# Cosine by the half angle, a shorter float64 conversion, and no whole tiles on GpSimd, in a fused attention and MoE kernel

## The chip, the core and the metric

The kernel runs on one core of a Trainium2 chip. Five engines with queues of their own are used: TensorE (PE for products, PEld for loading their stationary operand), VectorE (DVE), ScalarE (ACT), GpSimd (POOL) and SyncE (SP, which issues all transfers here). Each works through its instructions in the order in which they were issued, and they wait for each other at semaphores. The metric is the time of one execution on the device in microseconds.

## The reference

```python
def _attn_ref(q, k, v, g_norm):                       # float32, batch 8, 8 heads, 576 rows, 64 wide
    kv = np.einsum('bhsd,bhse->bhde', k, v)
    out = np.einsum('bhsd,bhde->bhse', q, kv)
    rms = np.sqrt(np.mean(out * out, axis=-1, keepdims=True) + 1e-06)
    return (out / rms * g_norm).astype(np.float32)

def _moe_ref(x, w_in, w_out):                         # x: 4608 x 512 (the heads side by side)
    h = x @ w_in                                      # w_in: 512 x 2048, float64
    g = h * np.cos(h)
    return (g @ w_out).astype(np.float32)             # w_out: 2048 x 512, float64
```

The weights reach the kernel as float64, the rest as float32.

## The kernel before

The 4608 tokens are cut into 12 chunks of 384, the 2048 hidden columns into 16 tiles of 128. A *step* is one such tile for one chunk: 192 steps. A step multiplies w_in's tile with the chunk's x (stage 1, into a PSUM bank `ps_h`), computes g = h cos(h) from it (`act_part`), and multiplies g with w_out's tile (stage 2, into three PSUM banks `acc`). Every float32 operand of the large products is split into a high part in float32r and a low part (the remainder), and three products are summed: so a step has 12 products of 384 columns into `ps_h` and 9 of 512 columns into `acc`. The names tell the parts: `xhi`/`xlo`, `ghi`/`glo`, and for a weight tile `wi` or `wo` its two halves `w[:, 0]` and `w[:, 1]`.

Four places matter here.

*Weights* (`w_part`, 32 tiles of 128x512). A tile lands as 64-bit words. DVE scales and clamps the low word (`m`), joins it by a shift and an or with the high word, and fixes sign and exponent bits. ACT makes the sign of the value from the high word in two operations (`sg`). The product of the two is the float32 value; ACT casts it to the high half, and the remainder is subtracted. Product and subtraction go to DVE or to POOL.

*Cosine* (`act_part`, per step). ACT makes `ki`, h over 2 pi plus a quarter, rounded to an integer by the int32 output. DVE subtracts ki times 2 pi in two parts (`r`), and clamps r. ACT takes the sine of r plus pi/2, DVE multiplies with h, ACT casts to `ghi`, and DVE or POOL subtracts to `glo`.

*x* (`x_part`, `kv_part`). For each chunk and pair of heads q is multiplied with k-transposed-v (`kv`) and normalised; the reciprocal root is a power on POOL (`rinv`) in a tile of 128x6 or 128x12. The remainders `qlo`, `xlo` and, for the early kv, `kv_lo` go to DVE or POOL. The first two chunks take a path with fewer transfers.

*Output* (`out_part`). ACT copies `acc` to SBUF and it is stored. The first two chunks use the first 8 tiles of the hidden columns, both of them, before the other 8, so their partial sums go out and come back, and DVE adds them.

The order of all instructions is made by a planner (`Order`) when the program is built: each part says which engine it needs next and for how long, the planner simulates the engines and issues an instruction when its simulated engine takes it; the lowest priority number goes first. Where a part names two engines, the one that would be done first is taken. `either(f, bias)` is such a choice between DVE and POOL:

```python
    def either(f, bias=0.0):
        return [("DVE", 0.067 + f / 960, bias), ("POOL", 0.15 + f / 480, 0.0)]
```

On the chip the order is fixed, the times are what they are. Every instruction is recorded by one helper, so the profile has line 190 for nearly all of them, and rows are told apart by their tiles.

Of the kernel before, what the change touches and what calls it, by code (L numbers as in the profile page):

```python
# [19 lines left out]
P = 128  # L20
# [29 lines left out]
class Order:  # L50
    """Puts the program's parts in an order by a simulation of the engines.

    A part of the program is a generator. It yields what it needs next: ("run", [(engine, us), ...], prio)
    for the use of one of these engines, ("wait", events) or ("take", tokens). After a "run" it issues its
    instructions, in the order in which the simulated engines start them; the lowest prio goes first.
    """
# [7 lines left out]

    def spawn(self, gen, t=0.0):
        self.advance(Proc(gen, t), None)

# [72 lines left out]
def tile_kernel(  # L140
# [271 lines left out]
    def kv_split_part(b, p, prio):  # L412
        """The parts of an early kv, for a chunk that isn't."""
# [3 lines left out]
        e, end = yield "run", either(P), prio  # L417
        by_name[e].tensor_tensor(
# [19 lines left out]
    def x_part(c, p, prio):  # L438
# [24 lines left out]
        else:  # L463
# [4 lines left out]
            e, end = yield "run", either(CH), prio  # L468
            by_name[e].tensor_tensor(out=qlo, in0=qT, in1=qhi.bitcast(F32), op=ALU.subtract)
# [85 lines left out]
        e, end = yield "run", either(CH), prio  # L555
        by_name[e].tensor_tensor(out=xlo[:, p, :], in0=x, in1=xhi[:, p, :].bitcast(F32), op=ALU.subtract)
# [4 lines left out]
    def w_part(key, prio):  # L561
        yield "wait", [w_in[key]]
        yield "take", t_wst
        sign_done = Event()
# [34 lines left out]
        e, end = yield "run", either(DM, 1.5), prio  # L599
        by_name[e].tensor_tensor(out=w[:, 1, :], in0=sg, in1=w[:, 0, :].bitcast(F32), op=ALU.subtract)  # L600
# [39 lines left out]
    def act_part(i, h):  # L640
        prio = due(i + 2) - 4.0
        yield "take", t_ki
        yield "run", [("ACT", 0.37)], prio
# [3 lines left out]
        yield "run", [("DVE", 0.47)], prio  # L647
        r = ew.tile([P, CH], F32, name="r")
        dve.scalar_tensor_tensor(out=r, in0=ki, scalar=-C1, in1=h, op0=ALU.mult, op1=ALU.add)
        _, end = yield "run", [("DVE", 0.47)], prio  # L650
        dve.scalar_tensor_tensor(out=r, in0=ki, scalar=-C2, in1=r, op0=ALU.mult, op1=ALU.add)
        sched.give(t_ki, end)
        yield "run", [("DVE", 0.27)], prio
        dve.tensor_scalar(
            out=r, in0=r, scalar1=-R_MAX - PI / 2, scalar2=R_MAX - PI / 2, op0=ALU.max, op1=ALU.min)
        yield "run", [("ACT", 0.51)], prio
        act.activation(out=r, in_=r, func=AF.Sin, bias=half_pi)
        _, end = yield "run", [("DVE", 0.47)], prio
# [3 lines left out]
        yield "run", [("ACT", 0.41)], prio  # L662
# [153 lines left out]
```

## Time and profile before

| what | value |
|---|---|
| times of three runs | 936.47, 937.34, 938.5 us (median 937.34) |
| profiled execution | span 933.4 us, first to last instruction; its own time is shown as this span alone |
| PE busy | 898.7 us (96%) |
| DVE busy | 722.4 us (77%) |
| ACT busy | 487.0 us (52%) |
| POOL busy | 221.2 us (24%), 105.4 of them powers |
| granted TensorE clock | 0.985 in the mean |

A row of a group reads: line, engine, operation, output and inputs by name, shape and type, count, then busy us and mean ns of one, then the idle time before them and what ended it. A row of the timeline reads: start in us, duration in us, engine, line, operation, names, shapes, count. A row of the waits reads: the engine and the tile that waited, for whom, us in total, times, longest.

### The profile page before, as it was taken

The page shows a single profiled execution, that of the slowest core. Times are in us where ns is not written, and L with a number is a line of the kernel's source. Part 1 is how long each engine was busy: PE and PEld are TensorE (multiplying, and loading weights), DVE is VectorE, ACT ScalarE, POOL GpSimd, SP SyncE. Part 2 cuts the span into 40 slices and gives each one's busy share as a digit, 9 for nine tenths or more (in the row PEclk, how much of TensorE's full clock was granted, in tenths as well). Part 3 has the DMA queues.
Part 4 walks back from the last instruction along what each step waited for, and adds up shares of the span by engine and source line. Part 5 has one row for each costly group of instructions (what it writes and reads, how often), then busy time and mean ns, then how long its engine had stood idle before and what let it go on. Part 6 is the DMA issues. An engine that isn't in the chain of part 4 may idle for free.

```text
span 933.4 us, 14111 instructions
## 1 busy us (share of the span) xinstructions
PE 898.7 (96%) x5008; PEld 798.7 (86%) x5008; DVE 722.4 (77%) x1442; ACT 487.0 (52%) x1094; POOL 221.2 (24%) x148
## 2 busy tenths in 40 slices
PE   8797878999999999999999999999999999999998
PEld 6685666889889998888889999889889999999997
DVE  3999999799777777777776876786886886886664
ACT  5876666455445445455445545454553653653443
POOL 3676655122120220121120220210210220220000
PEclk7899999999999999999999999999999999999999
DMA  9997001153211102121220111220310110100000
GB/s 253 261 314 233 35 0 57 18 161 99 68 42 43 18 9 69 43 60 47 58 67 25 27 18 30 72 69 9 94 18 1 51 18 1 52 1 1 35 1 34
DMA packets 112246, 58.59 MB, mean 63 GB/s; under 512 B 80432, under 2 KB 103984, under 8 KB 112176
## 3 DMA queue, kind: packets, MB, share of 16 engines
q1 hardware_dynamic: 112176, 57.70, 22.9%
q8 instruction: 39, 0.64, 0.3%
q14 instruction: 31, 0.25, 0.1%
HBM read 46.66 MB, written 11.01 MB: 62 GB/s over the span
## 4 chain that ended last, share of the span: by engine, by line
PE 83%; DVE 10%; DMA 3%; issue 1%; SPq 1%; ACT 0%; DVEq 0%
PE acc L190 39%; PE ps_h L190 39%; PE ps_a L190 5%; DVE m L190 4%; DVE r L190 3%; DVE glo L190 2%; DMA wo<-in_moe_w_out_dram 2%; DMA wi<-in_moe_w_in_dram 1%; SPq L364 1%; DMA wo<-in_v_dram 1%; SPq L321 1%; DVE xlo L190 0%; DVE sg L190 0%; DVE s L190 0%; SPq L348 0%
## 5 line engine op out<-in xcount | busy, mean ns | idle before, releaser
L190 PE MATMUL ps_h<-xhi,wi 128*128 128x384 f32 x1536 | 398.2, 340 | 8.8 <-DVE r L190 7.7
L190 PE MATMUL acc<-wo,ghi 128*128 128x512 f32 x1152 | 363.4, 397 | 1.0 <-ACT ghi L190 0.7
L190 PEld LDWEIGHTS ps_h<-xhi,wi 128*128 128x128 f32 x1536 | 282.5, 190 | 26.3 <-DVE r L190 10.2
L190 PE MATMUL ps_h<-xlo,wi 128*128 128x384 f32 x768 | 259.8, 338 | 0.0
L190 PEld LDWEIGHTS acc<-wo,ghi 128*128 128x128 f32 x1152 | 212.2, 189 | 37.7 <-ACT ghi L190 1.6
L190 PE MATMUL acc<-wo,glo 128*128 128x512 f32 x576 | 229.6, 399 | 11.2 <-DVE glo L190 11.1
L190 POOL TENSOR_TENSOR rinv<-ms,mhalf 128x12 f32<-128x12 f32 (+1 forms) x48 | 105.4, 2197 | 443.3 <-DVE ms L190 296.0
L190 ACT ACTIVATE r<-r,half_pi 128x384 f32<-128x384 f32 x192 | 117.9, 615 | 144.4 <-DVE r L190 143.2
L190 DVE TENSOR_TENSOR glo<-r,ghi 128x384 fp32r<-128x384 f32 x192 | 116.6, 608 | 44.0 <-ACT ghi L190 38.6
L190 DVE SCALAR_TENSOR_TENSOR r<-ki,ps_h 128x384 f32<-128x384 int32 x192 | 104.9, 547 | 59.1 <-ACT ki L190 57.7
L190 PEld LDWEIGHTS ps_h<-xlo,wi 128*128 128x128 f32 x768 | 145.1, 189 | 0.0
L190 DVE TENSOR_TENSOR r<-ps_h,r 128x384 f32<-128x384 f32 x192 | 106.1, 553 | 50.2 <-ACT r L190 49.5
L190 PEld LDWEIGHTS acc<-wo,glo 128*128 128x128 f32 x576 | 108.6, 189 | 40.0 <-DVE glo L190 16.5
L190 ACT ACTIVATE ki<-ps_h 128x384 int32<-128x384 f32 x192 | 94.0, 490 | 93.1 <-PE ps_h L190 92.1
L190 ACT CAST ghi<-r 128x384 fp32r<-128x384 f32 x192 | 98.1, 512 | 76.6 <-DVE r L190 75.6
L190 DVE SCALAR_TENSOR_TENSOR r<-ki,r 128x384 f32<-128x384 int32 x192 | 121.0, 631 | 3.1
L190 DVE TENSOR_SCALAR r<-r 128x384 f32<-128x384 f32 x192 | 75.1, 392 | 3.8
L190 POOL TENSOR_TENSOR sg<-m,sg 128x512 f32<-128x512 f32 x28 | 38.7, 1383 | 38.6 <-DVE m L190 24.1
L190 ACT CAST xhi<-s 128x384 fp32r<-128x384 f32 x45 | 23.1, 513 | 47.1 <-DVE s L190 47.0
L190 POOL TENSOR_TENSOR qlo<-qT,qhi 128x384 fp32r<-128x384 f32 x18 | 20.3, 1125 | 93.4 <-ACT qhi L190 72.5
L190 ACT COPY swp<-part 32x12 f32<-32x12 f32 x160 | 31.8, 199 | 11.4 <-DVE part L190 9.2
L190 ACT ACTIVATE s<-ps_a 128x384 f32<-128x384 f32 x45 | 21.9, 486 | 14.8 <-PE ps_a L190 14.6
(104 smaller groups left out, 639.0 us busy)
## 6 DMA issues: line engine op xcount, KB each, us to landing
out_dram<-ob SPq DMA_DIRECT2D x35, 256.0 KB, 2.1
wi<-in_moe_w_in_dram SPq DMA_DIRECT2D x16, 512.0 KB, 8.4
wo<-in_moe_w_out_dram SPq DMA_DIRECT2D x16, 512.0 KB, 9.8
kt<-in_k_dram SPq DMA_DIRECT2D x24, 256.0 KB, 2.8
vt<-in_v_dram SPq DMA_DIRECT2D x24, 256.0 KB, 3.1
qb<-in_q_dram SPq DMA_DIRECT2D x112, 48.0 KB, 2.1
qb<-in_q_dram SPq DMA_DIRECT2D x96, 24.0 KB, 1.8
part<-ob SPq DMA_DIRECT2D x6, 256.0 KB, 2.1
```

Of the source, the lines that this page charges most:

```text
L190: return lambda *a, **kw: tc.keep_in_program_order(f(*a, **kw))
L321: nc.sync.dma_start(out=t, in_=src[b, 2 * p:2 * p + 2].rearrange("h (p i) d -> p h i d", p=SF))
L364: nc.sync.dma_start(out=t, in_=src)
```

## The change

It edits four things, and the planner's costs with them.

- *Cosine.* cos(a) = 1 - 2 sin(a/2)^2, so g = -2 (sin(r/2)^2 - 0.5) h. `ki` loses its quarter and r its clamp; the sine takes r with scale 0.5 and no pointer operand; ACT squares; DVE subtracts 0.5 and multiplies with h in one operation. The factor -2 moves to the output: into ACT's copy and into DVE's addition.
- *Weights.* ACT scales the high word, read as float32, into a float32 (`sg`), and ACT or DVE scales the low word into an integer (`m`). DVE shifts `sg`'s bits and joins `m`, then takes the sign bit from the high word and joins it. That is the float32 value; the cast and the subtraction follow as before.
- *GpSimd.* `either` is gone; the remainders `glo`, `xlo`, `qlo`, `kv_lo` and those of the weights are all on DVE. POOL keeps the powers and the first fills.
- *Planner.* The durations that parts name are larger; a check that all parts have ended is added; comments are gone.

```diff
-    def either(f, bias=0.0):
-        return [("DVE", 0.067 + f / 960, bias), ("POOL", 0.15 + f / 480, 0.0)]
+    def dve_only(f):
+        return [("DVE", 0.15 + f / 960)]
...
-        def sign_part():
-            yield "run", [("ACT", 0.52)], prio
-            tiles["sg"] = wst.tile([P, DM], F32, name="sg")
-            act.activation(out=tiles["sg"].bitcast(I32), in_=words(F32, 1), func=AF.Copy, scale=HV_SCALE)
-            _, end = yield "run", [("ACT", 0.52)], prio
-            act.activation(out=tiles["sg"], in_=tiles["sg"].bitcast(I32), func=AF.Sign)
...
-        dve.tensor_scalar(
-            out=m, in0=words(U32, 0), scalar1=2.0 ** -29, scalar2=7.0, op0=ALU.mult, op1=ALU.min)
-        yield "run", [("DVE", 0.602)], prio
-        dve.scalar_tensor_tensor(
-            out=m, in0=words(I32, 1), scalar=3, in1=m,
-            op0=ALU.logical_shift_left, op1=ALU.bitwise_or)
-        yield "run", [("DVE", 0.335)], prio
-        dve.tensor_scalar(
-            out=m, in0=m, scalar1=0x7fffffff, scalar2=0x40000000, op0=ALU.bitwise_and, op1=ALU.bitwise_xor)
-        e, _ = yield "run", either(DM, 1.5), prio
-        by_name[e].tensor_tensor(out=sg, in0=m.bitcast(F32), in1=sg, op=ALU.mult)
+        def low_part():
+            e, end = yield "run", [("ACT", 0.67, 0.5), ("DVE", 0.63, 0.0)], prio
+            tiles["low"] = wst.tile([P, DM], I32, name="m")
+            if e == "ACT":
+                act.activation(out=tiles["low"], in_=words(U32, 0), func=AF.Copy, scale=LW_SCALE)
+            else:
+                dve.tensor_scalar(
+                    out=tiles["low"], in0=words(U32, 0), scalar1=LW_SCALE, scalar2=None, op0=ALU.mult)
...
+        act.activation(out=w32, in_=words(F32, 1), func=AF.Copy, scale=HW_SCALE)
+        yield "wait", [low_done]
+        yield "run", [("DVE", 0.69)], prio
+        dve.scalar_tensor_tensor(
+            out=wi, in0=wi, scalar=3, in1=tiles["low"], op0=ALU.logical_shift_left, op1=ALU.bitwise_or)
+        yield "run", [("DVE", 0.86)], prio
+        dve.scalar_tensor_tensor(
+            out=wi, in0=words(I32, 1), scalar=-2 ** 31, in1=wi, op0=ALU.bitwise_and, op1=ALU.bitwise_or)
...
-        e, end = yield "run", either(DM, 1.5), prio
-        by_name[e].tensor_tensor(out=w[:, 1, :], in0=sg, in1=w[:, 0, :].bitcast(F32), op=ALU.subtract)
+        _, end = yield "run", dve_only(DM), prio
+        dve.tensor_tensor(out=w[:, 1, :], in0=sg, in1=w[:, 0, :].bitcast(F32), op=ALU.subtract)
...
-        act.activation(out=ki, in_=h, func=AF.Copy, scale=INV_2PI, bias=0.25)
+        act.activation(out=ki, in_=h, func=AF.Copy, scale=INV_2PI)
...
-        dve.tensor_scalar(
-            out=r, in0=r, scalar1=-R_MAX - PI / 2, scalar2=R_MAX - PI / 2, op0=ALU.max, op1=ALU.min)
-        act.activation(out=r, in_=r, func=AF.Sin, bias=half_pi)
-        dve.tensor_tensor(out=r, in0=h, in1=r, op=ALU.mult)
+        act.activation(out=r, in_=r, func=AF.Sin, scale=0.5)
+        act.activation(out=r, in_=r, func=AF.Square)
+        dve.scalar_tensor_tensor(out=r, in0=r, scalar=0.5, in1=h, op0=ALU.subtract, op1=ALU.mult)
...
-            dve.tensor_tensor(out=o, in0=o, in1=acc, op=ALU.add)
+            dve.scalar_tensor_tensor(out=o, in0=acc, scalar=-2.0, in1=o, op0=ALU.mult, op1=ALU.add)
...
-            act.copy(out=o, in_=acc)
+            act.activation(out=o, in_=acc, func=AF.Copy, scale=-2.0)
```

How the instructions stand. First POOL's queue between the first powers (`rinv`), where the weights of the first steps are made; numbers behind names are buffers. Before:

```order
L190 TENSOR_TENSOR sg_268<-m_266,sg_268 128x512
L190 TENSOR_TENSOR wi1_344<-sg_268,wi1_344 128x512
L190 TENSOR_TENSOR rinv_384<-ms_381,mhalf_137 128x6
L190 TENSOR_TENSOR rinv_402<-ms_395,mhalf_137 128x6
L190 TENSOR_TENSOR wi2_404<-sg_322,wi2_404 128x512
L190 TENSOR_TENSOR wo0_415<-sg_386,wo0_415 128x512
L190 TENSOR_TENSOR kv_lo_92<-wo15_142,kv_hi_91 128x128
```

and after:

```order
L196 MEMSET kv_lo_92 128x1024
L196 TENSOR_TENSOR rinv_236<-ms_232,mhalf_136 128x6
L196 TENSOR_TENSOR rinv_309<-ms_306,mhalf_136 128x6
L196 TENSOR_TENSOR rinv_373<-ms_368,mhalf_136 128x6
L196 TENSOR_TENSOR rinv_400<-ms_395,mhalf_136 128x6
```

Only the powers are left. Second, DVE's queue around the first two `glo`. Before:

```order
L190 TENSOR_SCALAR r_523<-r_523 128x384
L190 TENSOR_SCALAR r_540<-r_540 128x384
L190 TENSOR_SCALAR m_502<-m_502 128x512
L190 TENSOR_SCALAR m_572<-wo2_469 128x512
L190 TENSOR_TENSOR r_523<-ps_h_329,r_523 128x384
L190 TENSOR_TENSOR r_540<-ps_h_406,r_540 128x384
L190 SCALAR_TENSOR_TENSOR m_572<-wo2_469,m_572 128x512
L190 TENSOR_TENSOR glo_587<-r_523,ghi_586 128x384
L190 TENSOR_TENSOR glo_594<-r_540,ghi_593 128x384
```

and after:

```order
L196 SCALAR_TENSOR_TENSOR r_516<-r_516,ps_h_323 128x384
L196 SCALAR_TENSOR_TENSOR sg_541<-sg_541,m_549 128x512
L196 SCALAR_TENSOR_TENSOR sg_471<-wi4_431,sg_471 128x512
L196 TENSOR_TENSOR glo_568<-r_516,ghi_567 128x384
L196 SCALAR_TENSOR_TENSOR r_547<-r_547,ps_h_391 128x384
L196 SCALAR_TENSOR_TENSOR sg_541<-wo2_444,sg_541 128x512
L196 TENSOR_TENSOR wi4_590<-sg_471,wi4_590 128x512
L196 TENSOR_TENSOR glo_604<-r_547,ghi_603 128x384
L196 TENSOR_TENSOR wo2_613<-sg_541,wo2_613 128x512
```

The clamps and the one-operand words are gone; two bit operations and the remainder of each weight stand between the steps. Third, ACT's queue from the fifth w_in tile (`wi4`) to the first sine. Before:

```order
L190 ACTIVATE sg_504<-wi4_446 128x512
L190 ACTIVATE ki_510<-ps_h_329 128x384
L190 ACTIVATE ki_520<-ps_h_406 128x384
L190 CAST wi3_525<-sg_441 128x512
L190 ACTIVATE sg_504<-sg_504 128x512
L190 CAST wo1_545<-sg_467 128x512
```

and after:

```order
L196 ACTIVATE sg_471<-wi4_431 128x512
L196 ACTIVATE m_487<-wi4_431 128x512
L196 COPY qhi_498<-ps_a_466 128x384
L196 COPY wo15_141<-ps_a_473 64x64 x2
L196 ACTIVATE ki_505<-ps_h_323 128x384
L196 CAST wi3_511<-sg_418 128x512
L196 CAST wo1_518<-sg_438 128x512
```

The low word's scaling (`m`) has come into ACT's queue ahead of the first `ki`, and the sign (`sg` from `sg`) is gone.

More of the change, by code (lines that the diff above doesn't have):

```diff
@@ L26 @@
 C2 = 2.0 * PI - C1
-R_MAX = 3.1415925
-HV_SCALE = 0.5 * 2.0 ** 15 / 1.125 * (1.0 + 2.0 ** -20)
+HW_SCALE = 2.0 ** -112
+LW_SCALE = 0.936 * 2.0 ** -29
 class Event:
@@ L63, in __init__ @@
         self.seq = 0
+        self.live = set()
     def spawn(self, gen, t=0.0):
-        self.advance(Proc(gen, t), None)
+        proc = Proc(gen, t)
+        self.live.add(proc)
+        self.advance(proc, None)
     def advance(self, proc, value):
@@ L202, in copy @@
             dve.tensor_copy(out=out, in_=in_)
-    def either(f, bias=0.0):
-        return [("DVE", 0.067 + f / 960, bias), ("POOL", 0.15 + f / 480, 0.0)]
+    def dve_only(f):
+        return [("DVE", 0.15 + f / 960)]
     kv_hi = const.tile([P, 2, NP, P], F32R, name="kv_hi")
     kv_lo = const.tile([P, 2, NP, P], F32R, name="kv_lo")
-    half_pi = const.tile([P, 1], F32, name="half_pi")
-    pool.memset(half_pi, PI / 2)
     warm = const.tile([P, 1], F32, name="warm")
-    act.activation(out=warm, in_=half_pi, func=AF.Sin)
+    pool.memset(warm, 0.0)
+    act.activation(out=warm, in_=warm, func=AF.Sin)
     zeros = const.tile([P, P], BF16, name="zeros")
@@ L416, in kv_split_part @@
         act.copy(out=kv_hi[:, b % 2, p, :], in_=kv_front[:, b, p, :])
-        e, end = yield "run", either(P), prio
-        by_name[e].tensor_tensor(
+        _, end = yield "run", dve_only(P), prio
+        dve.tensor_tensor(
             out=kv_lo[:, b % 2, p, :], in0=kv_front[:, b, p, :], in1=kv_hi[:, b % 2, p, :].bitcast(F32),
@@ L467, in x_part @@
             act.copy(out=qhi, in_=qT)
-            e, end = yield "run", either(CH), prio
-            by_name[e].tensor_tensor(out=qlo, in0=qT, in1=qhi.bitcast(F32), op=ALU.subtract)
+            _, end = yield "run", dve_only(CH), prio
+            dve.tensor_tensor(out=qlo, in0=qT, in1=qhi.bitcast(F32), op=ALU.subtract)
             sched.give(t_qT, end)
@@ L554, in x_part @@
         act.copy(out=xhi[:, p, :], in_=x)
-        e, end = yield "run", either(CH), prio
-        by_name[e].tensor_tensor(out=xlo[:, p, :], in0=x, in1=xhi[:, p, :].bitcast(F32), op=ALU.subtract)
+        _, end = yield "run", dve_only(CH), prio
+        dve.tensor_tensor(out=xlo[:, p, :], in0=x, in1=xhi[:, p, :].bitcast(F32), op=ALU.subtract)
         sched.give(t_xn, end)
@@ L589, in w_part @@
-        dve.tensor_scalar(
-            out=m, in0=m, scalar1=0x7fffffff, scalar2=0x40000000, op0=ALU.bitwise_and, op1=ALU.bitwise_xor)
-        yield "wait", [sign_done]
-        e, _ = yield "run", either(DM, 1.5), prio
-        sg = tiles["sg"]
-        by_name[e].tensor_tensor(out=sg, in0=m.bitcast(F32), in1=sg, op=ALU.mult)
-        yield "run", [("ACT", 0.52)], prio
+        def low_part():
[6 more added lines that the diff above has]
+                    out=tiles["low"], in0=words(U32, 0), scalar1=LW_SCALE, scalar2=None, op0=ALU.mult)
+            sched.fire(low_done, end)
@@ new lines, in w_part @@
+        _, end = yield "run", [("ACT", 0.67)], prio
+        sched.spawn(low_part(), end - 0.67 - sched.LAT)
+        w32 = wst.tile([P, DM], F32, name="sg")
+        act.activation(out=w32, in_=words(F32, 1), func=AF.Copy, scale=HW_SCALE)
+        yield "wait", [low_done]
+        yield "run", [("DVE", 0.69)], prio
+        wi = w32.bitcast(I32)
+        dve.scalar_tensor_tensor(
+            out=wi, in0=wi, scalar=3, in1=tiles["low"], op0=ALU.logical_shift_left, op1=ALU.bitwise_or)
+        yield "run", [("DVE", 0.86)], prio
@@ L596, in w_part @@
+        dve.scalar_tensor_tensor(
+            out=wi, in0=words(I32, 1), scalar=-2 ** 31, in1=wi, op0=ALU.bitwise_and, op1=ALU.bitwise_or)
+        sg = w32
+        yield "run", [("ACT", 0.62)], prio
         del w_raw[key]
@@ L642, in act_part @@
         yield "take", t_ki
[L643 removed]
+        yield "run", [("ACT", 0.485)], prio
         ki = ew.tile([P, CH], I32, name="ki", bufs=2)
[L645 removed]
+        act.activation(out=ki, in_=h, func=AF.Copy, scale=INV_2PI)
         yield "take", t_r
[L647 removed]
+        yield "run", [("DVE", 0.55)], prio
         r = ew.tile([P, CH], F32, name="r")
         dve.scalar_tensor_tensor(out=r, in0=ki, scalar=-C1, in1=h, op0=ALU.mult, op1=ALU.add)
[L650 removed]
+        _, end = yield "run", [("DVE", 0.55)], prio
         dve.scalar_tensor_tensor(out=r, in0=ki, scalar=-C2, in1=r, op0=ALU.mult, op1=ALU.add)
         sched.give(t_ki, end)
[L653 to L659 removed]
+        yield "run", [("ACT", 0.5)], prio
+        act.activation(out=r, in_=r, func=AF.Sin, scale=0.5)
+        yield "run", [("ACT", 0.5)], prio
+        act.activation(out=r, in_=r, func=AF.Square)
+        _, end = yield "run", [("DVE", 0.55)], prio
+        dve.scalar_tensor_tensor(out=r, in0=r, scalar=0.5, in1=h, op0=ALU.subtract, op1=ALU.mult)
         sched.give(t_h, end)
         yield "take", t_g
[L662 removed]
+        yield "run", [("ACT", 0.5)], prio
         ghi = ew.tile([P, CH], F32R, name="ghi")
@@ L665, in act_part @@
         act.copy(out=ghi, in_=r)
-        e, end = yield "run", either(CH, -0.5), prio
-        by_name[e].tensor_tensor(out=glo, in0=r, in1=ghi.bitcast(F32), op=ALU.subtract)
+        _, end = yield "run", dve_only(CH), prio
+        dve.tensor_tensor(out=glo, in0=r, in1=ghi.bitcast(F32), op=ALU.subtract)
         sched.give(t_r, end)
@@ L786, in tile_kernel @@
     sched.run()
+    assert not sched.live, sorted({x.gen.__name__ for x in sched.live})
 _INS = ['q', 'k', 'v', 'g_norm', 'moe_w_in', 'moe_w_out']
```

8 lines of the change are left out of this document (2 added, 6 removed).

## The prediction

> **What bounds the kernel now.** I read the 40 slices first, then busy time by stretch, then the waits, then the groups of the one stretch that is left over.
>
> ```profile
> PE   8797878999999999999999999999999999999998
> DVE  3999999799777777777776876786886886886664
> ```
>
> ```profile
> 37.00:60.00 23.00, 17.71 (x137) 15.50 (x136) 23.00 (x38) 16.09 (x35) 17.90 (x14) 0.79 1.08 320
> 60.00:164.00 104.00, 83.67 (x385) 68.15 (x384) 102.53 (x158) 68.66 (x133) 63.68 (x45) 0.96 0.30 95
> 164.00:200.00 36.00, 36.00 (x211) 32.16 (x212) 29.24 (x64) 18.07 (x44) 6.89 (x4) 1.00 0.29 80
> 200.00:880.00 680.00, 680.00 (x3781) 612.31 (x3781) 517.05 (x1086) 339.39 (x792) 114.86 (x62) 1.00 0.16 41
> ```
>
> After length, the columns are the busy us of PE, PEld, DVE, ACT and POOL, then PE's clock and DMA. From 164 us on PE has no gap: nothing done to DVE, ACT or POOL can shorten that part. From 37 to 164 us it is the other way round. DVE is busy 125.5 of 127 us, PE only 101.4. What PE waits for there (first two rows, waits from 40 to 170 us), and what it waits for later (last row, from 170 us to the end):
>
> ```profile
> PE acc L190 <- DVE glo L190: 11.1, 10, 2.6
> PE ps_h L190 <- DVE r L190: 7.7, 6, 2.8
> ...
> PEld acc L190 <- DVE glo L190: 0.2, 1, 0.2
> ```
>
> So the front is bound by DVE, the rest by PE. What the front could give at most: PE's idle there is 25.6 us (5.3 before 60 us, 20.3 after), and the clock granted below 1 costs about 0.21 x 23 = 4.8 and 0.04 x 104 = 4.2 us more. PE's own work in the 127 us is thus about 92 us at full clock.
>
> DVE has so much to do because its instructions are stretched. In the even part of the trace, a POOL whole tile starts at 405.90 and the DVE instruction after it ends when POOL's time and its own have passed one after the other:
>
> ```profile
> 405.05 0.56 DVE L190 SCALAR_TENSOR_TENSOR r<-ki,ps_h 128x384 f32<-128x384 int32 x1
> 405.52 0.55 DVE L190 TENSOR_TENSOR glo<-r,ghi 128x384 fp32r<-128x384 f32 x1
> 405.99 1.37 DVE L190 SCALAR_TENSOR_TENSOR r<-ki,r 128x384 f32<-128x384 int32 x1
> ...
> 408.25 0.56 DVE L190 SCALAR_TENSOR_TENSOR r<-ki,r 128x384 f32<-128x384 int32 x1
> ```
>
> ```profile
> 398.56 2.27 POOL L190 TENSOR_TENSOR rinv<-ms,mhalf 128x12 f32<-128x12 f32 x1 [17.14 <-DVE ms L190]
> 405.90 1.04 POOL L190 TENSOR_TENSOR qlo<-qT,qhi 128x384 fp32r<-128x384 f32 x1 [5.07 <-ACT qhi L190]
> ```
>
> The power that POOL keeps (rinv) does not do it: inside its 2.27 us a glo, with both operands in SBUF as well, took 0.56 us:
>
> ```profile
> 400.07 0.56 DVE L190 TENSOR_TENSOR glo<-r,ghi 128x384 fp32r<-128x384 f32 x1 [0.58 <-ACT ghi L190]
> ```
>
> From 37 to 165 us, by group:
>
> ```profile
> L190 DVE TENSOR_TENSOR glo<-r,ghi 128x384 fp32r<-128x384 f32 x20 | 20.4, 1024 | 0.6 <-ACT ghi L190 0.6
> L190 DVE SCALAR_TENSOR_TENSOR r<-ki,r 128x384 f32<-128x384 int32 x21 | 19.1, 912 | 0.0
> L190 DVE TENSOR_SCALAR m<-m 128x512 int32<-128x512 int32 x26 | 15.4, 598 | 0.0
> L190 DVE SCALAR_TENSOR_TENSOR m<-wi,m 128x512 int32<-128x512 int32 x12 | 15.1, 1255 | 0.1
> L190 DVE SCALAR_TENSOR_TENSOR m<-wo,m 128x512 int32<-128x512 int32 x14 | 12.3, 880 | 0.0
> ...
> L190 DVE TENSOR_SCALAR m<-wo 128x512 int32<-128x512 uint32 x14 | 10.2, 726 | 0.0
> L190 DVE TENSOR_SCALAR r<-r 128x384 f32<-128x384 f32 x20 | 8.8, 442 | 0.0
> L190 DVE TENSOR_SCALAR m<-wi 128x512 int32<-128x512 uint32 x11 | 6.9, 624 | 0.0
> L190 DVE TENSOR_TENSOR xlo<-s,xhi 128x384 fp32r<-128x384 f32 x4 | 5.0, 1260 | 0.0
> ...
> L190 DVE TENSOR_TENSOR sg<-m,sg 128x512 f32<-128x512 f32 x2 | 2.0, 998 | 0.0
> ```
>
> Unstretched, the same kinds take (DVE first, then ACT):
>
> ```profile
> 49.02 0.42 DVE L190 TENSOR_SCALAR m<-wo 128x512 int32<-128x512 uint32 x1
> 49.36 0.35 DVE L190 TENSOR_SCALAR r<-r 128x384 f32<-128x384 f32 x1
> 49.63 0.68 DVE L190 SCALAR_TENSOR_TENSOR m<-wi,m 128x512 int32<-128x512 int32 x1
> 50.23 0.68 DVE L190 SCALAR_TENSOR_TENSOR m<-wo,m 128x512 int32<-128x512 int32 x1
> ```
>
> ```profile
> 49.39 0.67 ACT L190 ACTIVATE sg<-wo 128x512 int32<-128x512 f32 x1
> 49.96 0.60 ACT L190 ACTIVATE r<-r,half_pi 128x384 f32<-128x384 f32 x1
> 50.47 0.60 ACT L190 CAST wo<-sg 128x512 fp32r<-128x512 f32 x1
> 50.98 0.63 ACT L190 ACTIVATE sg<-sg 128x512 f32<-128x512 int32 x1
> 51.51 0.49 ACT L190 COPY s<-rinv 128x384 f32<-128x384 f32 x1
> 51.91 0.51 ACT L190 CAST ghi<-r 128x384 fp32r<-128x384 f32 x1
> ```
>
> Count x (mean minus plain): glo 20 x 0.47 = 9.4, r<-ki,r 21 x 0.36 = 7.6, m<-m 26 x 0.18 = 4.7, the two shifts 12 x 0.575 + 14 x 0.20 = 9.7, the two low words 14 x 0.31 + 11 x 0.20 = 6.5, clamp 20 x 0.09 = 1.8, xlo 4 x 0.71 = 2.8. Together 42 us of stretch, so DVE's own work is 125.5 - 42 = 83 us.
>
> **The change, part by part.** The front has 20 steps and 26 weights. For occupancy I use start to start, since neighbours overlap: on DVE 0.34 (one operand, 512), 0.27 (clamp), 0.60 (two operands, 512); on ACT 0.57 (word scaled), 0.51 (sine), 0.51 (cast), 0.53 (sign), 0.40 (384 copy).
>
> Whole tiles off GpSimd: 42 us of stretch go. On DVE the weights' remainders come in: two of 26 are there already, so 24 x 0.60 = +14.4; the products with the sign vanish from both engines (two on DVE, -1.2). Three kv_lo of 128x128, about 0.2 us each by scaling the 0.55 of 384: +0.6.
>
> Weights: the 26 m<-m and 25 low words leave DVE, 51 x 0.34 = -17.3; 26 second bit operations come, priced as the shift, whose operands are of the same kinds: +15.6. ACT scales the low word (0.57) in place of taking the sign (0.53): 26 x 0.04 = +1.
>
> Cosine: the clamp goes, 20 x 0.27 = -5.4; the last product keeps its form. ACT gets a square per step. The trace has none with both ends in SBUF; bounds are the 0.40 of the copy and the 0.51 of the sine. I take 0.40, the nearer in kind: +8.0. The sine loses its pointer operand; I count nothing for that.
>
> So for the same work DVE needs 83 + 14.4 - 1.2 + 0.6 - 17.3 + 15.6 - 5.4 = 90 us, ACT 84.8 + 1 + 8 = 94 us, PE 92 us, against 127 now. Three engines nearly level replace one overloaded one, and each works in a fixed order, so the stretch won't shrink to 94. Before 60 us I leave the 10 us that PE loses now (idle and clock): loads and the first x are late there, not DVE alone. ACT's queue is no better there: the scaled words of wi4 (now two, not one) stand ahead of the first step's ki and wait for this landing (from the chain that ended last), at 35.2 us:
>
> ```profile
> 26.47 8.72 DMA wi<-in_moe_w_in_dram
> ```
>
> DVE's first bit operation now waits for both words from ACT, and the r and glo of steps are queued behind it; PE waits for those. After 60 us I let the loss fall from 24.5 to 4 us, for the handovers. 92 + 10 + 4 = 106, a gain of 21 us. Ends: with the loss before 60 us halved and none after, 97 (gain 30). If neighbours did not overlap at all, DVE would take 26 x 3 x 0.68 + 20 x 4 x 0.56 + about 7 (the second chunk's x: the four xlo, as many products, small ones) = 105, ACT about as much (26 x 1.94 + 20 x 2.1 + the x), and with 10 us of start the stretch takes 115 (gain 12).
>
> From 164 us on: per step DVE loses 0.27 and ACT gains 0.40; DVE also gets the qlo and xlo that POOL had. ACT is busy 339 of 680 us there and DVE 517, so both stay covered by PE. The outputs' factor -2 rides on a copy and an addition that are there already, and costs nothing under the same cover. The chain from a finished h to glo gets a square (0.40 to 0.51) for a clamp (0.35). If that cover is gone, PE waits at glo in each step; the wait there is 0.2 us in all now.
>
> POOL's power stands behind no whole tile any more. That can bring the first x forward; I count nothing.
>
> A rule against this change: the Trainium skill, "Perfetto Trace Analysis", Optimizing Scalar/DVE Operations, says that work may be moved off a saturated DVE to ScalarE or even GpSimd, though with the caution that the two share a port. Read by its first half, the change goes the wrong way, and the time would be the 938 of the third rival below; by the 405.99 row it is 916.
>
> **Rivals.** The profiled execution spans 933.4 us, and the median of the runs, 937.3, is 3.9 above; I carry that over. Forecast: 937.3 - 21 = 916.
>
> 1. The levelled engines lose more. If ACT, now the fullest, stalls DVE and PE with its queue, 5 to 10 us less are won: 921 to 930. For it: 94 us of ACT in a stretch of 106. Against: ACT has 42 us free there now.
> 2. PE waits in the even part: slower. The longer chain makes PE wait at glo in 168 steps. It outweighs the front's 21 us from 0.13 us a step on; with 0.2 us a step it is 34 - 21 = +13, 950. For it: the chain grows by up to 0.16 us. Against: the 0.2 us row, and DVE has fewer instructions there.
> 3. DVE's instructions are long by themselves. Then removed and added ones go by their stretched means: 125.5 - 15.4 - 17.1 - 8.8 - 2.0 + 26 x 1.05 + 24 x 0.68 + 0.6 = 126.4, and nothing is won: 938. Against: 0.56 and 1.37 for one instruction within 3 us.
> 4. Better: the pow and the unstretched DVE bring the first x forward too, 904 to 907.
>
> **Numbers.** Forecast (907 to 925, the range of its own ends) 0.72; rival 1 beyond that 0.13; rival 4 0.06; rival 3 0.04; rival 2 0.05. No change means within 0.2%, about 1.9 us, which is what a measurement can tell here. Faster: 0.72 + 0.13 + 0.06 = 0.91; same 0.04; slower 0.05. A range from 904 to 928 leaves out rivals 2 and 3, the upper part of rival 1 and the fringes, together some 0.2.
>
> **What would show it.** Right: in 37 to 150 us the means of glo and r<-ki,r fall to about 0.56, POOL holds only powers, DVE is below 90% and ACT above 80% there, and PE is without gap from about 143 us on. Wrong: glo still at 1 us (rival 3); PE waits on ACT ghi or r in the front (1); waits on glo after 200 us (2). The square at more than 0.51 us would spoil ACT's term.

## The result and the profile after

The changed kernel takes 911.88 us in the median (909.66 to 914.87) against 937.12 us in the runs beside it (936.47 to 938.5): a ratio of 0.9732, 95% interval 0.9713 to 0.9752, or 25.2 us less. The profiled execution spans 909.9 us against 933.4, so 23.5 of these are in the trace.

The slices of PE and DVE, from the page of the changed kernel:

```profile
PE   8799998999999999999999999999999999999998
DVE  3779889877767767767766766776766776766553
```

The second to the seventh slice of DVE, all 9 before, are 7, 7, 9, 8, 8 and 9 now. By stretch (after length: busy us of PE, PEld, DVE, ACT, POOL, then PE's clock and DMA), changed kernel:

```profile
37.00:60.00 23.00, 18.68 (x134) 16.13 (x134) 17.98 (x35) 20.13 (x47) 3.34 (x2) 0.93 1.06 311
60.00:164.00 104.00, 98.72 (x510) 86.80 (x509) 90.59 (x176) 83.97 (x176) 2.96 (x2) 1.00 0.35 106
37.00:164.00 127.00, 117.40 (x642) 102.94 (x642) 108.57 (x210) 104.09 (x222) 6.29 (x4) 0.99 0.48 143
164.00:905.00 741.00, 740.16 (x4095) 665.81 (x4094) 502.60 (x1031) 427.09 (x1014) 92.17 (x40) 1.00 0.16 41
```

and the front stretch of the kernel before, for the same window as the third row:

```profile
37.00:164.00 127.00, 101.38 (x519) 83.65 (x519) 125.53 (x195) 84.74 (x168) 81.58 (x59) 0.93 0.44 136
```

In these 127 us PE did 117.4 x 0.99 = 116 us of full-clock work where it did 101.4 x 0.93 = 94 before: 22 of the 23.5 us. DVE went from 99% to 85% busy, ACT from 67% to 82%. From 164 us on PE has 0.8 us of idle in 741; the longer ACT work is hidden there. The groups of the front stretch (37 to 165 us), changed kernel:

```profile
L196 DVE SCALAR_TENSOR_TENSOR sg<-sg,m 128x512 int32<-128x512 int32 x26 | 17.8, 685 | 2.1 <-ACT m L196 2.1
...
L196 DVE TENSOR_TENSOR glo<-r,ghi 128x384 fp32r<-128x384 f32 x26 | 14.4, 553 | 0.5 <-ACT ghi L196 0.3
L196 DVE SCALAR_TENSOR_TENSOR r<-ki,r 128x384 f32<-128x384 int32 x26 | 14.3, 552 | 0.0
```

glo has gone from 1024 to 553 ns, r<-ki,r from 912 to 552, and DVE now waits a little for ACT. PE's own waits, 40 to 170 us:

```profile
PE ps_h L196 <- DVE r L196: 3.6, 3, 1.7
...
PE acc L196 <- ACT ghi L196: 1.9, 2, 1.5
```

The 11.1 us of waiting on glo are gone. The 20th step's glo, in the timelines of before and after:

```profile
162.24 1.59 DVE L190 TENSOR_TENSOR glo<-r,ghi 128x384 fp32r<-128x384 f32 x1 [0.58 <-ACT ghi L190]
```

```profile
138.10 0.55 DVE L196 TENSOR_TENSOR glo<-r,ghi 128x384 fp32r<-128x384 f32 x1
```

It starts 24.1 us earlier, about as much as the span is shorter: the gain is made by then.

### The profile page after: what moved, and what is told of

Its sections match the earlier page's. It is cut to its first block, busy times and chain, and to the rows that moved or that the text cites. A ratio compares the mean times of both kernels' runs of the same rounds, so it can differ in the third digit from the quotient of the medians.

```text
span 909.9 us, 13803 instructions
## 1 busy us (share of the span) xinstructions
PE 892.2 (98%) x5008; PEld 797.2 (88%) x5008; DVE 629.2 (69%) x1276; ACT 553.5 (61%) x1283; POOL 107.6 (12%) x61
## 4 chain that ended last, share of the span: by engine, by line
PE 90%; DMA 3%; DVE 3%; SPq 1%; ACT 1%; issue 1%; POOL 0%; ACTq 0%; DVEq 0%
PE acc L196 43%; PE ps_h L196 42%; PE ps_a L196 5%; DMA wo<-in_moe_w_out_dram 1%; DMA wi<-in_moe_w_in_dram 1%; DVE r L196 1%; DVE sg L196 1%; DMA out_dram<-ob 1%; DMA wo<-in_v_dram 1%; SPq L324 1%; SPq L367 0%; DVE wi L196 0%; DVE glo L196 0%; POOL rinv L196 0%; ACT ki L196 0%
## 5 line engine op out<-in xcount | busy, mean ns | idle before, releaser
L196 ACT ACTIVATE r<-r 128x384 f32<-128x384 f32 x384 | 200.4, 524 | 81.5 <-DVE r L196 76.6
L196 PE MATMUL acc<-wo,glo 128*128 128x512 f32 x576 | 227.2, 394 | 0.1
L196 DVE SCALAR_TENSOR_TENSOR r<-r,ps_h 128x384 f32<-128x384 f32 x192 | 105.4, 550 | 60.0 <-ACT r L196 59.4
L196 DVE TENSOR_TENSOR glo<-r,ghi 128x384 fp32r<-128x384 f32 x192 | 105.7, 551 | 23.9 <-ACT ghi L196 22.3
L196 DVE SCALAR_TENSOR_TENSOR r<-ki,r 128x384 f32<-128x384 int32 x192 | 105.9, 552 | 2.3
L196 DVE STREAM_TRANSPOSE s<-s 128x384 f32<-128x384 f32 x40 | 23.1, 578 | 41.0 <-ACT s L196 40.7
L196 DVE STREAM_TRANSPOSE s<-rinv 128x384 f32<-128x384 f32 x40 | 23.0, 575 | 11.2 <-POOL rinv L196 11.1
L196 DVE TENSOR_TENSOR xlo<-s,xhi 128x384 fp32r<-128x384 f32 x45 | 25.0, 555 | 6.8 <-ACT xhi L196 4.9
```

The source lines that it names most:

```text
L196: return lambda *a, **kw: tc.keep_in_program_order(f(*a, **kw))
```

## The experiments

The theory was the prediction's: POOL's whole tiles stretch DVE's instructions, DVE bounds the front, PE the rest. "Before" was 935.6 to 936.4 us in the medians beside these runs.

### Which of the three parts carries it

Six kernels fill the table of old and new weights, old and new cosine, and POOL with or without its choice of whole tiles.

**POOL's choice alone.** The kernel before, with both uses of the choice sent to DVE:

```diff
-        return [("DVE", 0.067 + f / 960, bias), ("POOL", 0.15 + f / 480, 0.0)]
+        return [("DVE", 0.067 + f / 960, bias)]
```

> The kernel before with every remainder and every sign product on DVE (POOL keeps the powers); cosine, conversion and planner costs as before. Theory (whole tiles on POOL stretch DVE, about 42 us for 52 of them in the front, 0.8 us each): 48 instructions of 0.60 us come to DVE, +29, and 42 go, so the front is about 13 us shorter: 924 us (919 to 930), and the mean of glo in the front falls from 1024 ns to about 560. Rival A (DVE's instructions are long by themselves, the shorter arithmetic made the gain): 29 us more for an engine that is busy 125.5 of 127 us: 945 us or more. Rival B (the planner's new costs made the gain): about 937.

Measured: 920.37 us, ratio 0.9835 (0.98 to 0.987). In the groups of 37 to 165 us:

```profile
L190 DVE TENSOR_TENSOR sg<-m,sg 128x512 f32<-128x512 f32 x28 | 18.8, 681 | 0.0
...
L190 DVE TENSOR_TENSOR glo<-r,ghi 128x384 fp32r<-128x384 f32 x23 | 12.6, 550 | 0.5 <-ACT ghi L190 0.5
```

The stretch is gone (glo 550 ns), though DVE now makes 28 products there that POOL nearly all made before. DVE is busy 122.6 of 127 us and the kernel is still 15 us faster.

**The cosine alone.** The kernel before with the half-angle cosine:

```diff
-        dve.tensor_scalar(out=r, in0=r, scalar1=-R_MAX - PI / 2, ...)
-        act.activation(out=r, in_=r, func=AF.Sin, bias=half_pi)
-        dve.tensor_tensor(out=r, in0=h, in1=r, op=ALU.mult)
+        act.activation(out=r, in_=r, func=AF.Sin, scale=0.5)
+        act.activation(out=r, in_=r, func=AF.Square)
+        dve.scalar_tensor_tensor(out=r, in0=r, scalar=0.5, in1=h, op0=ALU.subtract, op1=ALU.mult)
```

> The kernel before with the cosine alone changed (no clamp, half angle, square on ACT, the factor -2 at the output). Theory: DVE loses 20 clamps of 0.27 to 0.44 us in the front, 5 to 9 us: 928 to 932. Rival A: the same or a little more, 926 to 930. Rival B: 937. If the longer chain costs anything after the front, PE waits on glo appear after 200 us.

Measured: 934.07 us, ratio 0.9981 (0.9963 to 0.9999). A miss: nearly nothing. Its groups, 37 to 165 us:

```profile
L190 DVE SCALAR_TENSOR_TENSOR r<-ki,r 128x384 f32<-128x384 int32 x21 | 22.0, 1053 | 0.1
L190 DVE TENSOR_TENSOR glo<-r,ghi 128x384 fp32r<-128x384 f32 x20 | 18.1, 907 | 1.9 <-ACT ghi L190 1.9
L190 DVE TENSOR_SCALAR m<-m 128x512 int32<-128x512 int32 x27 | 17.7, 657 | 0.1
```

The clamps are gone, but POOL's tiles hit other instructions instead: r<-ki,r rose from 912 to 1053 ns and m<-m from 598 to 657, while glo fell from 1024 to 907. Counted over all groups of this window as in the prediction (count times mean minus plain), the stretch is an estimated 42 us again, with 51 whole tiles on POOL. A stretched instruction that is removed takes only its own time with it; the stretch belongs to POOL's tile.

**The weights alone.** The kernel before with the new conversion; POOL may still take the remainders:

```diff
-        dve.tensor_scalar(out=m, in0=words(U32, 0), scalar1=2.0 ** -29, scalar2=7.0, ...)
...
-        by_name[e].tensor_tensor(out=sg, in0=m.bitcast(F32), in1=sg, op=ALU.mult)
+        act.activation(out=w32, in_=words(F32, 1), func=AF.Copy, scale=HW_SCALE)
+        dve.scalar_tensor_tensor(out=wi, in0=wi, scalar=3, in1=tiles["low"], ...)
+        dve.scalar_tensor_tensor(out=wi, in0=words(I32, 1), scalar=-2 ** 31, in1=wi, ...)
```

> The kernel before with the conversion of the weights alone changed (the remainder may still go to POOL; the sign product on POOL is gone with the old conversion). Theory: 26 whole tiles fewer on POOL in the front, stretch 42 to 21 us, DVE's own work 83 - 17.3 + 15.6 - 1.2 = 80: DVE needs 101, the front 20 to 25 us less: 912 to 919. Rival A (no stretch by POOL): DVE 125.5 - 15.4 - 17.1 - 2.0 + 27.4 = 118, 930. Rival B: 937.

Measured: 915.2 us, ratio 0.9779 (0.9754 to 0.9804), as the theory had it. The product with the sign, POOL's work before, does not exist any more, so POOL's busy time in 37 to 164 us falls from 81.6 to 48.1 us without anything being moved.

**The changed kernel with POOL's choice back.**

```diff
-            _, end = yield "run", dve_only(DM), prio
-            dve.tensor_tensor(out=w[:, 1, :], in0=sg, in1=w[:, 0, :].bitcast(F32), op=ALU.subtract)
+            e, end = yield "run", either(DM, 1.5), prio
+            by_name[e].tensor_tensor(out=w[:, 1, :], in0=sg, in1=w[:, 0, :].bitcast(F32), op=ALU.subtract)
```

> The changed kernel with the choice between DVE and POOL for remainders put back (the planner then gives POOL all 32 weights' remainders, 32 qlo, 12 xlo, 1 glo). Theory: 26 whole tiles in the front stretch DVE by 0.8 us each, 21 us, and take 26 x 0.60 = 15.6 us from it: DVE needs about 95 in place of 90, the front 3 to 8 us more: 915 to 920 us; glo's mean in the front is between 560 and 1024 ns. Rival A: DVE has 15.6 us less to do, 905 to 912. Rival B: 912.

Measured: 911.74 us, ratio 0.9738 (0.9713 to 0.9764). The same was done for glo, xlo, qlo and kv_lo. A miss: no loss at all, though the stretch is back (groups of 37 to 165 us, then 60 to 164 us):

```profile
L196 DVE SCALAR_TENSOR_TENSOR sg<-sg,m 128x512 int32<-128x512 int32 x27 | 24.9, 933 | 0.0
L196 DVE SCALAR_TENSOR_TENSOR r<-ki,r 128x384 f32<-128x384 int32 x26 | 24.1, 931 | 0.0
```

```profile
60.00:164.00 104.00, 102.53 (x553) 91.13 (x548) 100.00 (x164) 83.37 (x175) 44.23 (x30) 1.00 0.36 111
```

DVE is busy 100 of 104 us from 60 us on, and PE 102.5: DVE is full and PE is fed all the same. POOL did all 32 weights' remainders. By the theory's own prices each costs DVE 0.8 us of stretch (42 us for 52 tiles) and saves it 0.60 of its own. DVE's busy time from 37 to 164 us rose from 108.6 to 120.5 us (low words came to it as well), but in this order, made with the longer durations, PE waited for DVE only 2.3 us there. Its longest wait was 6.1 us for ACT, before 60 us.

**The changed kernel with the old cosine, and with the old weights** (the parts above undone; POOL without whole tiles):

> The changed kernel with the old cosine back (turn added on ScalarE, clamp on VectorE, one sine, plain product); weights new, GpSimd without whole tiles. Between the kernel before with VectorE alone (920.4 us) and the changed kernel (911.9). Theory: VectorE no longer bounds the stretch once the weights are new (114 of 127 us busy even with 20 clamps of 0.35 us added, ScalarE 8 us less), so the cosine is worth little here: 909 to 915. Rival A, the clamp's VectorE time is on the path: 915 to 920. Rival B, the square on ScalarE costs more than the clamp did: under 909.

> The changed kernel with the old float64 conversion back (clamped low word, shift, two bit operations, sign and product); cosine new, GpSimd without whole tiles. Theory: VectorE loses 22 x 0.69 us in the front stretch again and is its bound: 915 to 920, near the kernel before with VectorE alone (920.4). Rival, the cosine alone carries the gain: 909 to 914.

Measured: 923.18 us, ratio 0.9864 (0.9839 to 0.9889), and 923.43 us, ratio 0.9861 (0.9839 to 0.9883). Both are misses, above what the theory gave: the first by 8 us, beyond its rival A too, the second by 3. All medians together:

| us | POOL may take whole tiles | POOL takes none |
|---|---|---|
| old weights, old cosine | 936 (a) | 920.4 (a) |
| old weights, new cosine | 934.1 (a) | 923.4 (b) |
| new weights, old cosine | 915.2 (a, the weights' own b) | 923.2 (b) |
| new weights, new cosine | 911.7 (b) | 911.9 (b) |

The planner's durations are those of the kernel before in (a) and the longer ones of the changed kernel in (b), and they matter by themselves (last group of experiments), so only entries with the same letter are compared. Of these: POOL's tiles gone are worth 15 us in the kernel before and nothing in the changed one. The cosine is worth 2 us in the kernel before and 11 in the changed one, the weights 11 in the changed one. The parts do not add up. Where the time lies is seen in PE by three stretches; the kernel before, the changed one, and the one with the old cosine, in this order:

```profile
37.00:90.00 53.00, 41.95 (x262) 36.07 (x262) 52.45 (x84) 37.14 (x78) 37.67 (x28) 0.90 0.95 286
90.00:130.00 40.00, 32.19 (x143) 26.14 (x142) 40.00 (x62) 27.02 (x51) 25.73 (x18) 0.96 0.05 20
130.00:164.00 34.00, 27.24 (x118) 21.44 (x117) 33.08 (x51) 20.58 (x40) 18.18 (x14) 0.95 0.11 39
```

```profile
37.00:90.00 53.00, 46.62 (x278) 40.49 (x278) 45.28 (x90) 46.75 (x104) 6.29 (x4) 0.97 0.96 287
90.00:130.00 40.00, 40.00 (x204) 36.43 (x203) 34.58 (x65) 33.70 (x71) 0.00 (x0) 1.00 0.16 54
130.00:164.00 34.00, 30.78 (x163) 26.02 (x163) 28.71 (x57) 23.64 (x49) 0.00 (x0) 1.00 0.10 24
```

```profile
37.00:90.00 53.00, 46.44 (x267) 41.41 (x266) 44.90 (x93) 41.90 (x90) 5.65 (x4) 0.90 0.89 282
90.00:130.00 40.00, 39.99 (x202) 35.92 (x201) 34.11 (x70) 27.56 (x54) 0.00 (x0) 1.00 0.13 47
130.00:164.00 34.00, 28.62 (x130) 24.07 (x130) 30.89 (x60) 23.01 (x44) 0.00 (x0) 0.95 0.04 10
```

In the middle stretch PE is full as soon as the DVE work is cut by either way. With the old cosine PE loses 2.2 us more than the changed kernel in the last stretch, and works at a lower clock in the first and the last (0.90 and 0.95 against 0.97 and 1.00). At 141 to 143 us PE waits 2.2 us for a ghi there. Its first product with glo starts at 47.8 us in the changed kernel and at 47.9 with the old cosine. From then on PE is idle some 5 us more: 1.6 up to 90 us, 2.2 in the last stretch, 1.7 from 164 to 250 us, and 0.5 less after that. The clock was 0.94 against 1.00 from 47.8 to 90 us and 0.95 against 1.00 in the last stretch, by which it lost another 3.7 or so. Together these are almost 9 of the 9.9 us between the two spans. The clock's part need not be the cosine's: the run with early fills below has the changed kernel's order on PE, and was granted 0.95 in the last stretch as well. DVE is not full in the last stretch (30.9 of 34), so it is not DVE's load alone; whether it is the clamp in the chain or the order that the planner made with it, these runs do not separate.

### Is it POOL's reading

**Reads put back.** The changed kernel, with four POOL products on each finished weight, written to a scratch that nobody reads. The order on PE, DVE and ACT stays as it was.

```diff
+        for _ in range(4):
+            pool.tensor_tensor(
+                out=scratch, in0=w[:, 0, 0:208].bitcast(F32), in1=w[:, 1, 0:208].bitcast(F32), op=ALU.mult)
```

> The changed kernel, and on POOL four products of two read halves of each finished weight into a scratch tile that nobody reads (128x208, 128 instructions in all); the order on PE, DVE and ACT is the same as without them. Theory (a POOL tile that reads SBUF holds up DVE's instructions with two operands there): DVE is stretched again by some 15 to 35 us in the front though nobody waits for POOL's results; r<-ki,r and glo go from 0.55 to 0.7 or more, and the time to 918 to 935 us. If DVE's longer times before came from waits for POOL's results or from the instructions themselves: 912, glo at 0.55.

**Fills in place of reads**, with one product of 8 columns ahead so that they start at the same places:

```diff
+        pool.tensor_tensor(out=scratch[:, 0:8], in0=w[:, 0, 0:8]..., in1=w[:, 1, 0:8]..., op=ALU.mult)
+        for _ in range(8):
+            pool.memset(scratch, 0.0)
```

> The same place, but POOL reads 8 columns of each weight and then writes the scratch tile eight times (fills, no reading). Theory, if it is the reading that holds DVE up: 912, r<-ki,r at 0.55 us. If any work of POOL does it: 914 to 920.

Measured: 934.43 us with the reads, ratio 0.9971 (0.9955 to 0.9987); 920.0 us with the fills, ratio 0.9828 (0.9806 to 0.985). The reads take back nearly the whole gain. Their timeline, where four products of a `wi` run one after the other:

```profile
85.27 0.68 DVE L196 SCALAR_TENSOR_TENSOR sg<-wo,sg 128x512 int32<-128x512 int32 x1
85.49 3.96 POOL L196 TENSOR_TENSOR scratch<-wi 128x208 bf16<-128x208 f32 x4 [2.86 <-DVE wi L196]
85.87 0.54 DVE L196 SCALAR_TENSOR_TENSOR r<-ki,ps_h 128x384 f32<-128x384 int32 x1
86.34 0.68 DVE L196 SCALAR_TENSOR_TENSOR sg<-sg,m 128x512 int32<-128x512 int32 x1
86.94 0.99 DVE L196 SCALAR_TENSOR_TENSOR r<-ki,r 128x384 f32<-128x384 int32 x1
87.85 1.12 DVE L196 TENSOR_TENSOR wo<-sg,wo 128x512 fp32r<-128x512 f32 x1
88.90 1.11 DVE L196 SCALAR_TENSOR_TENSOR sg<-wo,sg 128x512 int32<-128x512 int32 x1
```

r<-ki,ps_h, which reads one operand from PSUM, keeps its 0.54; the sg<-sg,m after it keeps its 0.68 too, and the next three, with two SBUF operands each, go from 0.55 to 0.99 and from 0.68 to 1.1: not every one is hit, but most. With the fills the DVE groups keep their length (glo 552 ns, sg<-sg,m 684 ns from 37 to 140 us), and still 8 us are lost, where the theory had 912: a miss. POOL's queue shows why:

```profile
70.04 0.17 DVE L196 TENSOR_SCALAR ms<-ps_a 128x6 f32<-128x6 f32 x1 [0.62 <-PE ps_a L196]
...
71.39 2.58 POOL L196 MEMSET scratch<- 128x208 bf16 x8
...
73.94 1.32 POOL L196 TENSOR_TENSOR rinv<-ms,mhalf 128x6 f32<-128x6 f32 x1
...
75.29 0.51 ACT L196 COPY s<-rinv 128x384 f32<-128x384 f32 x1 [4.05 <-POOL rinv L196]
...
75.86 0.55 PE L196 MATMUL ps_a<-ident,s 128*128 128x128 f32 x3 [3.33 <-ACT s L196]
```

The power could start at 70.2, when `ms` is done; it stands behind the product of 8 columns, which waits for its weight until 70.95, and behind eight fills, until 73.9. ACT, which works in order, waits 4.05 us for it, and PE 3.3 for ACT.

**The fills without that wait.** The product of 8 columns is left out; nothing holds the fills back, and they run as soon as POOL reaches them.

> The changed kernel with the same 8 GpSimd fills of 128x208 per weight as in the run with fills, but without the small product that made each group wait for its weight: the fills then run as soon as GpSimd's queue reaches them, and are mostly over when the next reciprocal root comes up. Theory (a fill lengthens no VectorE instruction; the 8 us of the run with fills were the reciprocal roots that stood in GpSimd's queue behind fills, with ScalarE and then TensorE waiting): 911 to 915, and TensorE's wait on the scaled states falls from 7.6 us to under 4. Rival (GpSimd's writes slow the others by themselves): 917 to 921.

Measured: 915.26 us, ratio 0.9788 (0.9759 to 0.9817); a little above the theory's 915. PE's wait on the scaled states is 1.5 us from 37 to 164 us, against 7.6 with the fills that waited. With 67 us of POOL work in the front stretch, 60.7 of them fills, glo takes 553 ns and PE is busy 117.39 of the 127 us, as in the changed kernel (117.40). Of the 2.5 us by which its span is longer, 2.3 are PE idle before 37 us. There one power still stands behind fills:

```profile
27.37 5.20 POOL L196 MEMSET scratch<- 128x208 bf16 x16
32.53 1.83 POOL L196 TENSOR_TENSOR rinv<-ms,mhalf 128x6 f32<-128x6 f32 x1
```

So POOL's writing costs DVE nothing; its reading does, and a long POOL queue does by itself. Of the 22.6 us that the reads cost, 14.4 are the difference to the fills at the same places; PE's wait on the scaled states is shorter with the reads (4.4 us against 7.6), so that wait does not make the difference. The Trainium skill, "SBUF — State Buffer", Who interferes with whom, says the same: a DVE instruction with two SBUF inputs contends with a GpSimd instruction that reads SBUF, not with one that only writes.

### ACT's margin

```diff
         act.copy(out=ghi, in_=r)
+        act.copy(out=ghi, in_=r)
```

> The changed kernel with ACT's cast to ghi done twice in each step (192 more instructions of 0.41 us, in the chain from h to glo). It asks how near ACT and the chain are to being the bound. By the terms of the prediction ACT's 94 us in the front become 102, and 0.4 us more in the chain is still covered after the front: 913 to 920, with new PE idle before 160 us only. If the chain had no room left after the front, 0.4 us in each of 168 steps would give up to 67 us more: 930 to 980.

Measured: 917.34 us, ratio 0.9795 (0.9779 to 0.981): 5.5 us for 192 further casts. ACT is then 114.6 of 127 us busy in the front, yet PE is busy 116.9 us there against 117.4; the 20th step's glo starts at 139.0 us, 0.9 later than in the changed kernel, and the 24th at 158.3, 2.3 later. So ACT had room in the front for most of the added work, and less than half of the 5.5 us is lost by its end. After 164 us PE has no wait on glo, but waits 2.1 us in all where ACT copies an output, against 0.7; the expectation had new idle before 160 us only. A chain longer by a cast of 0.51 us per step stays covered. Where the rest of the 5.5 us goes was not followed.

### The planner's durations

**Shorter ones.** The changed kernel, its durations set to the start-to-start times of the trace:

```diff
-        return [("DVE", 0.15 + f / 960)]
+        return [("DVE", 0.067 + f / 960)]
...
-            e, end = yield "run", [("ACT", 0.67, 0.5), ("DVE", 0.63, 0.0)], prio
+            e, end = yield "run", [("ACT", 0.57, 0.5), ("DVE", 0.34, 0.0)], prio
...
-        yield "run", [("DVE", 0.86)], prio
+        yield "run", [("DVE", 0.60)], prio
```

and likewise 0.69 to 0.60 and 0.55 to 0.47 on DVE, 0.62 to 0.52, 0.5 to 0.41 and 0.485 to 0.39 on ACT.

> The changed kernel with the planner's durations shortened to start-to-start values (DVE 0.47 and 0.60, ACT 0.41 and 0.57, about as before the change), so that only the order differs. Theory (the order matters little): 908 to 916. Rival B (the longer durations in the planner made part of the gain): 918 or more.

Measured: 905.05 us, ratio 0.9667 (0.9644 to 0.969): the fastest of all, 7 us ahead of the changed kernel. A miss: it lies below the theory's range (908 to 916), on the far side from the rival. Its front:

```profile
37.00:164.00 127.00, 122.77 (x689) 110.07 (x688) 115.98 (x229) 105.90 (x231) 9.13 (x6) 0.97 0.52 157
```

PE has 4.2 us of idle left there instead of 9.6. The longer durations of the change were a cost, not a gain.

**The same with POOL's choice back** (the edit of the choice, shown above, on top of it, with 0.067 in place of 0.15 in DVE's price):

> The changed kernel with the planner's shorter durations (905.05 us by themselves) and the choice of GpSimd for remainders back. Theory: as with the longer durations, what GpSimd takes off VectorE (some 30 weight remainders) and what its reads add to VectorE's other instructions cancel: 903 to 908. Rival A (the stretch is now so tight that reads by GpSimd cost): over 909. Rival B (VectorE at 116 of 127 us still holds the stretch, taking work off it gains): under 903.

Measured: 920.74 us, ratio 0.9841 (0.9811 to 0.9871): rival A, by more than it asked for.

```profile
37.00:164.00 127.00, 112.63 (x603) 98.17 (x602) 111.34 (x185) 90.24 (x187) 51.59 (x35) 0.95 0.44 136
```

DVE is less busy than without POOL (111 against 116 us), yet PE does 10 us less. The planner, which knows nothing of the stretch, found DVE so free at its 0.34 that it put 26 of the 32 low words there (11 without POOL, 16 with POOL and the longer durations). The groups of 37 to 164 us:

```profile
L196 DVE TENSOR_SCALAR m<-wo 128x512 int32<-128x512 uint32 x12 | 8.1, 686 | 0.0
...
L196 DVE TENSOR_SCALAR m<-wi 128x512 int32<-128x512 uint32 x8 | 4.4, 552 | 0.0
```

They took 552 and 686 ns in the mean, not 420. PE's largest wait is on `r`, 7.3 us, and ACT waits 13.8 us for it. So POOL's choice costs 16 us with the shorter durations, as it did 15 in the kernel before, and nothing with the longer ones. That the longer ones fit DVE as POOL stretches it (0.86 us for the second bit operation), and so make a better order exactly where POOL reads, would explain both; it is a reading, and no run separates the stretch from the order.

## Why the prediction came out as it did

*What bounds the kernel.* Right: 22 of 23.5 us came from 37 to 164 us, none after.

*The stretch from 127 to 106 us.* The 20th step's glo starts 101 us after 37 us now and started 125 after it before (the 127 ran on to 164 us): 24 us less, where I had 21. Of 92 + 10 + 4 one term was wrong. The 92 charged the low clock to PE's idle time too; by busy time and clock PE's work up to 164 us was 94, and up to 138 us in the changed kernel it is 92, so the term served. From 60 to 138 us PE was idle 3.4 us, near the 4. Before 60 us it lost 4.3 us of idle and 0.07 x 18.7 = 1.3 by its clock, 5.6 where I had left all 10; only the low end of my range had that halved. DVE's load and POOL's tiles are part of what was late there, and I had put it down mostly to landings: with POOL's choice alone taken away PE was idle 2.0 us in these 23, at full clock. Rival 4's mechanism had no part: PE's first product with glo starts at 47.8 us in both kernels. The fourth glo still comes later than before (66.4 us against 62.0), the sixth comes earlier (78.1 against 83.1).

*42 us of stretch go with POOL's tiles.* The mechanism is right (1024 to 553 ns; the reads bring it back, the fills don't). The step that failed is whose gain it is. I had the whole 42 us go by taking whole tiles off POOL. But the 26 products with the sign vanish with the new weights, wherever POOL's choice stands, and half of POOL's tiles with them. What the move of the remainders gains on top hangs on the planner's durations: nothing with those of the changed kernel (911.7 against 911.9), 16 us with shorter ones (920.7 against 905.05).

*The cosine.* I had 5.4 us less on DVE and 8 more on ACT, a wash. In the kernel before it was (2 us). In the changed kernel the old one costs 11 us. The traces show some 5 of these as PE's idle time and 3.7 as lower clock; why that order waits there stays open.

*DVE at 90, ACT at 94 us.* In 37 to 138 us DVE was busy 85.5 and ACT 86.2 us; the counts are lower (22 to 24 weights, 19 or 20 steps), since some weights were ready earlier. The square was priced 0.40 start to start and the sine kept at 0.51. The changed kernel's pair:

```profile
96.33 1.08 ACT L196 ACTIVATE r<-r 128x384 f32<-128x384 f32 x2 [0.61 <-DVE r L196]
97.31 0.65 ACT L196 ACTIVATE sg<-wi 128x512 f32<-128x512 f32 x1
```

Two in 97.31 - 96.33 = 0.98 where the square follows its own sine, against 0.51 for the old sine: 0.47 more per step, 0.07 above my term. Where another instruction stands between them, as in most steps of the front, it is less:

```profile
62.15 0.52 ACT L196 ACTIVATE r<-r 128x384 f32<-128x384 f32 x1
62.57 0.57 ACT L196 ACTIVATE s<-ps_a,gcol 128x384 f32<-128x384 f32 x1
63.03 0.52 ACT L196 ACTIVATE r<-r 128x384 f32<-128x384 f32 x1
63.44 0.62 ACT L196 CAST wi<-sg 128x512 fp32r<-128x512 f32 x1
```

The sine holds ACT for 0.42 and the square for 0.41, together 0.32 more than the old sine. Either way it is no matter for the sum. The mean of sine and square is 524 ns, the sine with the pointer operand 613 in the run with the old cosine. The 0.09 that I counted as nothing is real; the Trainium skill, "ScalarE: Activation LUTs", What ACT_TABLE_LOAD costs, gives about 93 ns for such an operand, and these rows agree.

*Rival 1, levelled engines.* It did not come. ACT was 82% busy, and with a second cast per step, at 90%, the 24th step's glo came 2.3 us later; the rest of the 5.5 us was lost after the front.

*Rival 2, waits in the even part.* No: PE's waits after 170 us have no row on glo, and even a second cast put none there.

*Rival 3, long by themselves.* No, by the 553 ns and by the run with POOL's choice taken away.

*The signs.* All of the right ones came: glo and r<-ki,r at 0.55, only powers on POOL, DVE at 85%, ACT at 82%, PE's last gap of more than half a microsecond in the front ending at 143.4 us. Of the wrong ones, the wait on ACT ghi showed weakly, 1.9 us in the front. The planner's durations, which the sum left out, were worth 7 us, more than the error of any of its three terms. That the time fell into the range is in part luck: it hangs on this loss, which the sum did not have; without it the time was 905 us, below the range's 907.

## What to carry to other kernels

Where two engines stretch each other, look first for work that can vanish from both; what a move from one to the other gains was 15 us or nothing here, by the order around it. Do not add up single edits of an order that a planner makes anew each time. Feed such a planner start-to-start times from the trace when no other engine stretches them (with POOL's choice back, the order from the shorter times was the slower one, 920.7 against 911.7 us), and see what PE waits for in the stretch, not how busy an engine is: with DVE at 100 of 104 us PE was fed, and at 111 of 127 it was not.

## What the runs showed of the hardware

POOL's fills, 60.7 us of them in the front, did not lengthen DVE's groups there, while 128x208 products that read SBUF took DVE's two-operand instructions from 0.55 to 0.99 and from 0.68 to 1.1 us. One-operand DVE instructions can be stretched as well when POOL reads: in the last run a low word that starts at 41.91 us, beside POOL's wi<-sg,wi, takes 1.48 us, one at 38.14 beside nothing 0.41, one at 48.41 beside a power 0.41. And PE's idle time is not the whole loss of a stretch: with 6.6 and 6.4 us of it from 37 to 90 us, the granted clock was 0.90 with the old cosine and 0.97 in the changed kernel, and 1.00 with 6.7 us of idle in the run with early fills, which has the changed kernel's order on PE; what sets it was not tried.
